# Attention with values as the moving operand and a column of ones, in a fused attention and soft mixture-of-experts kernel

## The chip, the cores and the metric

The kernel runs on one core of one Trainium2 chip. A core has five engines that run their own instruction streams in order: PE (TensorE, matrix multiply, writes PSUM only), DVE (VectorE), ACT (ScalarE), POOL (GpSimd, no access to PSUM) and SP (SyncE, which here only issues DMAs). The metric is device microseconds of one execution. In the profile PE is the stream of matmuls and PEld the stream of their weight loads, which run beside them.

## The reference

`q`, `k`, `v` are 8 batches x 8 heads x 576 positions x 64. Attention is done per head, then a soft mixture of experts on all 4608 rows:

```python
q_rot, k_rot = rotate(q), rotate(k)                  # rotary embedding
scores = 1/8 * q_rot @ k_rot.T                       # 576 x 576 per head
attn = exp(scores - max(scores, -1))
attn = attn / (sum(attn, -1) + 1e-9)
x = (attn @ v) -> rows (4608, 512)
logits = x @ phi                                     # 32 slots
d = softmax over rows (logits); c = softmax over slots (logits)
slot_input = d.T @ x                                 # 32 x 512
h = relu(slot_input[e] @ w1[e]); slot_out = h @ w2[e]
out = c @ slot_out
```

## The kernel before, in words

Two heads of one batch make a pair: head 0 on partitions 0 to 63, head 1 on 64 to 127. There are 32 pairs, four to a batch. For each pair these steps run, and the steps of several pairs overlap:

- `load0`, `load1` (SP): q and k of the pair, transposed, into `x_in` (two buffers). `spin` (POOL, 8 instructions): multiply by cosines and sines. `join` (DVE): add the two products. `high` (ACT, 2 instructions) and `low` (DVE): split into two f16 parts, `hl`. `low` is the last reader of `x_in`, so the load of the pair after next waits for it.
- `m00` to `m31` and `m_rem`: nine units that find the largest score of each query. PE computes scores from the high parts, DVE takes the maximum (L177, L185). `m_min` (DVE), `m_turn` (PE transposes, L200), `m_half` (ACT) and `m_rows` (a DMA) bring the negated maximum into a row, `peak`.
- `t0` to `t8`: nine score units. A unit is 64 keys x 576 queries of both heads in four terms (three products of the f16 parts, and the maximum through the constant `lift`), 16 matmuls of 64x64 stationary by 288 moving columns. ACT takes the exponential into `a_t` (L226).
- `av0` to `av8`: nine value units. Stationary is 64 keys x 64 columns of `v` in f32, moving is `a_t`, 288 columns. The result has head columns on partitions and queries along the row.
- `total`: the sums of the exponentials. DVE adds two groups of `a_t` into `c_t` (L252), PE multiplies by a 0/1 matrix `pick` (L263, 48 matmul passes of 128x32 stationary by 144 columns), ACT copies out (L269).
- `send`, `recip`, `spread`, `widen`: the sums go through small DMAs and DRAM to be spread over partitions, `norm` (POOL, L297) multiplies. The last two pairs do it on PE and DVE instead (`sums_turn`, `sums_wide`, L317, `norm_wide`).
- `natural` (PE, five transposes, L331 and L332) and `natural_out` (ACT) bring the rows into natural order, `xn`. Per batch: `logits` (L346), softmax statistics and the slot sums (L389 to L427).

Score units, maximum units, transposes and the like share three PSUM buffers of two banks (`ps_s`); the value result has one (`ps_o`).

The order on PE, ACT, DVE, SP and POOL is written out. `WHEN` gives every step of a pair a time in quarters of a pair; step s of pair p stands at `WHEN[s] + 4 * p`, and each engine takes its instructions in that order. A fixed list starts the first two pairs. Weights of the experts are loaded into free memory on the way; after the last pair come the statistics of the last batch, both expert layers and the output.

In PE's tables below 64\*64 or 128\*32 is rows x columns of the stationary tile. An f32 matmul is two passes, each with its own weight load, and each pass is one instruction in the profile.

Of the kernel before, what the change touches and what calls it, by code (L numbers as in the profile page):

```python
# [43 lines left out]
RC = 12  # L44
QC = HC // 2
PIECE = 4
NB = S // 64
GRP = 3
N_A = 3
WHEN = {  # L50
    "load0": -14.036, "load1": -13.155, "spin0": -11.12, "spin1": -11.002, "join": -8.686, "high0": -8.581,
    "high1": -8.145, "low": -7.119, "m01": -6.438, "m10": -6.296, "m00": -5.409, "m11": -4.37, "m21": -4.235,
    "m20": -3.955, "m30": -3.558, "load_v": -3.19, "m31": -2.689, "m_rem": -2.154, "m_min": -1.862, "m_turn":
# [5 lines left out]
    "recip": 4.894, "sums_wide": 5.348, "norm_wide": 5.483, "spread": 6.496, "natural_late": 6.717,  # L59
    "logits_late": 6.765, "logits_out_late": 6.993, "widen": 7.249, "natural_out_late": 7.405, "norm": 9.097,  # L60
    "natural": 11.079, "natural_out": 11.153, "logits": 11.213, "logits_out": 11.274, "stats": 12.331,
}
QL, QH, KH, KL = range(4)


@with_exitstack
# [884 lines left out]
```

## Time and profile before

| | |
|---|---|
| three runs | 551.47, 549.48, 551.17 us, median 551.17 |
| profiled execution | 549.75 us, span 548.0 us |
| busy PE, DVE, ACT, POOL | 515.7, 429.7, 311.6, 326.4 us |
| mean granted clock of PE | 0.98 |
| DMA | 111.35 MB, mean 203 GB/s |

A busy PE is not yet a PE at its limit, since an instruction lasts until its result is out while the next ones already stream: four 64\*64 matmuls of 288 columns last 0.29 us each, but a new set of four starts every 0.12 us. So the tables are read by the distance from start to start.

### The profile page before, as it was taken

The numbers are of one execution on the slowest core, as the hardware profiler recorded it, in microseconds if no ns is written. First come the engines' busy times: TensorE is split into PE (matmuls) and PEld (weight loads), VectorE is DVE, ScalarE is ACT, GpSimd is POOL, SyncE is SP. The second block draws the span as 40 slices with busy tenths as digits, with TensorE's granted clock in tenths as the row PEclk, the third lists the DMA queues.
The fourth block names the chain that finished last, engine by engine and source line by source line (L and its number), as shares of the span: only waits on it lengthen the run. The fifth ranks groups of instructions, "written<-read, shape, count | busy, mean of one in ns | idle before, by whom it ended". The sixth has DMA issues, their size and how long they took to land.

```text
span 548.0 us, 25344 instructions
## 1 busy us (share of the span) xinstructions
PE 515.7 (94%) x11325; PEld 389.2 (71%) x11325; DVE 429.7 (78%) x580; ACT 311.6 (57%) x655; POOL 326.4 (60%) x324
## 2 busy tenths in 40 slices
PE   4679999999999999999999999999999999999982
PEld 2267787877787777777887788777878886754551
DVE  5779998879998999899988998899889953232352
ACT  2146566666666666656675666566656665354441
POOL 1957787666886688668876887687678111210000
PEclk9689999999999999999999999999999999999997
DMA  7264566666566566556655665566434256459998
GB/s 263 93 216 134 193 194 193 193 192 193 194 194 193 192 192 195 190 183 202 196 195 159 220 197 195 169 204 206 138 120 121 70 182 218 169 190 411 407 417 343
DMA packets 51292, 111.35 MB, mean 203 GB/s; under 512 B 11504, under 2 KB 28656, under 8 KB 51184
## 3 DMA queue, kind: packets, MB, share of 16 engines
q1 hardware_dynamic: 51170, 109.73, 59.7%
q8 instruction: 89, 1.46, 1.1%
q14 instruction: 19, 0.16, 0.1%
q10 hardware_dynamic: 14, 0.00, 0.0%
HBM read 99.93 MB, written 9.58 MB: 200 GB/s over the span
## 4 chain that ended last, share of the span: by engine, by line
PE 87%; DVE 6%; DMA 4%; ACT 1%; issue 1%; SPq 0%; DVEq 0%; ACTq 0%
PE o_ps L238 26%; PE s_ps L225 26%; PE s_ps L263 9%; PE s_ps L175 6%; PE s_ps L331 3%; PE s_ps L789 3%; PE s_ps L346 2%; DVE nm L177 2%; DMA w_exp<-in_w 2%; PE s_ps L400 1%; PE s_ps L813 1%; PE s_ps L200 1%; DVE x_in L146 1%; DMA out<-w_exp 1%; PE s_ps L183 1%; DMA x_in<-in_qk 1%
## 5 line engine op out<-in xcount | busy, mean ns | idle before, releaser
L142 POOL TENSOR_TENSOR x_in<-x_in,cs_sb 128x288 f32<-128x288 f32 x248 | 254.5, 1063 | 80.8 <-DMA x_in<-in_qk 69.0
L226 ACT ACTIVATE a_t<-s_ps 128x576 f32<-128x576 f32 x288 | 179.6, 653 | 89.5 <-PE s_ps L225 89.2
L177 DVE TENSOR_REDUCE nm<-s_ps 128x2 f32<-128x576 f32 x256 | 183.0, 750 | 41.3 <-PE s_ps L175 39.5
L238 PE MATMUL o_ps<-a_t,v_in 64*64 64x288 f32 x2304 | 195.8, 408 | 0.0
L225 PE MATMUL s_ps<-hl 64*64 64x288 f16 x3456 | 166.5, 285 | 4.1 <-DVE nm L177 3.2
L225 PEld LDWEIGHTS <-hl 64*64 64x64 f16 x3456 | 124.6, 107 | 29.4 <-issue 6.5
L225 PE MATMUL s_ps<-peak,lift 64*64 64x288 f16 x1152 | 99.8, 284 | 0.3 <-issue 0.3
L238 PEld LDWEIGHTS o_ps<-a_t,v_in 64*64 64x64 f32 x2304 | 85.7, 133 | 8.2 <-issue 0.5
L175 PE MATMUL s_ps<-hl 64*64 64x288 f16 x1024 | 79.6, 290 | 4.1 <-DVE nm L177 4.0
L297 POOL TENSOR_TENSOR xt<-xt,rb 128x576 f32<-128x576 f32 x30 | 48.0, 1599 | 32.2 <-ACT a_t L226 13.1
L252 DVE TENSOR_TENSOR c_t<-a_t 128x1728 f32<-128x1728 f32 x32 | 62.8, 1961 | 0.0
L155 DVE TENSOR_TENSOR hl<-x_in,hl 128x1152 f16<-128x1152 f32 x32 | 60.1, 1880 | 0.5 <-ACT hl L151 0.5
L175 PEld LDWEIGHTS <-hl 64*64 64x64 f16 x1024 | 38.3, 106 | 24.7 <-issue 15.5
L146 DVE TENSOR_TENSOR x_in<-x_in 128x1152 f32<-128x1152 f32 (+2 forms) x36 | 55.3, 1535 | 0.1
L151 ACT CAST hl<-x_in 128x576 f16<-128x576 f32 (+1 forms) x66 | 40.1, 653 | 23.5 <-DVE x_in L146 21.6
L225 PEld LDWEIGHTS <-lift 64*64 64x64 f16 x1152 | 46.5, 107 | 0.7 <-issue 0.5
L337 ACT COPY xn<-s_ps 128x512 f32<-128x512 f32 x31 | 18.1, 583 | 29.1 <-PE s_ps L332 29.1
L420 POOL TENSOR_TENSOR ln<-ln,cm 128x160 f32<-128x160 f32 x7 | 14.7, 2096 | 32.4 <-DVE cm L419 32.4
L269 ACT ACTIVATE s<-s_ps,bits 128x144 f32<-128x144 f32 x32 | 12.2, 381 | 34.6 <-ACT xn L338 14.2
L263 PE MATMUL s_ps<-c_t,pick 128*32 128x144 f32 x768 | 30.4, 289 | 0.7 <-DVE c_t L252 0.5
L263 PE MATMUL s_ps<-a_t,pick 128*32 128x144 f32 x768 | 29.7, 286 | 0.0
L263 PEld LDWEIGHTS s_ps<-c_t,pick 128*32 128x32 f32 x768 | 21.1, 109 | 6.3 <-issue 4.7
(175 smaller groups left out, 463.7 us busy)
## 6 DMA issues: line engine op xcount, KB each, us to landing
x_in<-in_qk SPq DMA_DIRECT2D x62, 576.0 KB
w_exp<-in_w SPq DMA_DIRECT2D x63, 512.0 KB
v_in<-in_v SPq DMA_DIRECT2D x32, 576.0 KB
out<-w_exp SPq DMA_DIRECT2D x18, 512.0 KB
rb<-r_row SPq DMA_DIRECT2D x60, 144.0 KB
x_in<-in_qk SPq DMA_DIRECT2D x4, 288.0 KB
cs_sb<-in_cs SPq DMA_DIRECT2D x2, 288.0 KB
wk<-in_w SPq DMA_DIRECT2D x1, 512.0 KB
```

The lines of the kernel that those rows point to most:

```text
L142: eng.tensor_tensor(out=x[:, :, c], in0=x[:, :, c], in1=cs_sb[:, :, c], op=ALU.mult)
L146: nc.vector.tensor_tensor(out=x[:, t, 0, c], in0=x[:, t, 0, c], in1=x[:, t, 1, c], op=ALU.add)
L151: nc.scalar.copy(out=halves[p][:, 1 + t, c], in_=loaded[p][:, t, 0, c])
L155: nc.vector.tensor_tensor(out=hl[:, 0:4:3], in0=x[:, :, 0], in1=hl[:, 1:3], op=ALU.subtract)
L175: nc.tensor.matmul(s[rows[c ^ h], h, 0:HC], lhsT=hl[rows[h], QH, at:at + 64], rhs=hl[rows[h], KH, half[n]], start=True, stop=True)
L177: nc.vector.tensor_reduce(out=nms[p][:, n, j:8:4], in_=s[:, :, 0:HC], axis=AX.X, op=ALU.max, negate=True)
L225: nc.tensor.matmul(s[rows[h ^ n], n, 0:HC], lhsT=lhs, rhs=rhs, start=(x == 0), stop=(x == 3))
L226: nc.scalar.activation(out=ats[p, g][:, b].rearrange("p (n x) -> p n x", n=2), in_=s[:, :, 0:HC], func=AF.Exp, scale=SCALE)
L238: nc.tensor.matmul(o[rows[h], n, 0:HC], lhsT=vt[r, i, n], rhs=ats[p, g][r, b, half[n]], start=(i == 0), stop=(i == NB - 1))
L252: nc.vector.tensor_tensor(out=c, in0=ats[p, 0], in1=ats[p, 1], op=ALU.add)
L263: nc.tensor.matmul(s[32 * k:32 * k + 32, 0, 0:QC], lhsT=pick[:, 16 * n:16 * n + NS], rhs=(c, a)[x // GRP][:, x % GRP, QC * k:QC * k + QC], ...
L297: eng.tensor_tensor(out=xts[p], in0=xts[p], in1=rbs.pop(p), op=ALU.mult)
```

## The change

- Scores and maxima: the stationary tile has 128 columns (128 keys, or 128 queries for the maxima) in place of two of 64, so a unit has half as many matmuls. A score unit is now 128 keys x 288 queries; t0 to t7 cover 512 keys, t8 (`score_rest`) the last 64 keys in 64x64 tiles, with queries cut 320/256.
- Values: `a_t` (64 queries) is stationary and `v` moves, 64 columns and a column of ones, so that column 64 of the result is the sum of the exponentials. Units av0 to av3 are 128 keys deep (128\*64 tiles, 18 matmuls of 65 columns, two column halves), av4 is the last 64 keys (64\*64 tiles, 18 matmuls). The result has queries on partitions.
- `total`, `send`, `spread`, `widen` and their DMAs, the sum on DVE and the PE path of the last two pairs go. `o_out` is three ACT copies, `recip` three small DVE instructions, `norm` two POOL instructions that write `xn` directly. `natural` transposes `xn` to `xt` (five transposes of 128x128), for the logits only.
- `v` is laid out as 10 blocks of 65 columns on the host (325 KB a pair in place of 576 KB). `xn` has two buffers.
- All times in `WHEN` are new; the fixed start is now the table `EARLY` with the same steps. After the last pair `norm_last` divides straight from PSUM.

```diff
-    "load0": -14.036, "load1": -13.155, "spin0": -11.12, "spin1": -11.002, "join": -8.686, "high0": -8.581,
+    "load0": -13.475, "spin0": -13.456, "load1": -13.036, "spin1": -12.384, "join": -11.941, "high0": -11.78,
...
+    both = (slice(0, P),) if WIDE else rows
...
-        for c in range(2):
+        for c in both:
             for h in range(2):
-                at = P * j + 64 * (c ^ h)
-                nc.tensor.matmul(s[rows[c ^ h], h, 0:HC], lhsT=hl[rows[h], QH, at:at + 64],
+                nc.tensor.matmul(s[c, h, 0:HC], lhsT=hl[rows[h], QH, P * j + c.start:P * j + c.stop],
                                  rhs=hl[rows[h], KH, half[n]], start=True, stop=True)
...
+        for x, (k, q) in enumerate(TERMS):
+            for c in both:
+                for h in range(2):
+                    lhs = lift[rows[h], c] if k is None else hl[rows[h], k, P * b + c.start:P * b + c.stop]
+                    rhs = pk[rows[h], half[n]] if k is None else hl[rows[h], q, half[n]]
+                    nc.tensor.matmul(s[c, h, 0:HC], lhsT=lhs, rhs=rhs, start=(x == 0), stop=(x == 3))
+        nc.scalar.activation(out=ats[p, b][:, :, half[n]], in_=s[:, :, 0:HC], func=AF.Exp, scale=SCALE)
...
-        for n in range(2):
-            for h in range(2):
-                r = rows[h ^ n]
-                nc.tensor.matmul(o[rows[h], n, 0:HC], lhsT=vt[r, i, n], rhs=ats[p, g][r, b, half[n]],
-                                 start=(i == 0), stop=(i == NB - 1))
+        def unit(lhs, c, h, u, v, stop=False):
+            nc.tensor.matmul(o[rows[c], h, 65 * u:65 * u + 65], lhsT=lhs, rhs=v, start=(i == 0 and u == first), stop=stop)
+
+        if i < NB:
+            first = 0
+            for c, h, u in [(c, h, u) for u in range(4) for h in range(2) for c in range(2)] + [(0, 0, 4), (1, 1, 4)]:
+                q = 256 if u == 4 else 64 * u + 320 * c
+                unit(at[:, h, q:q + 64], c, h, u, vt[:, 2 * i + h])
...
+        nc.scalar.copy(out=t.rearrange("p h u x -> p h (u x)")[:, :, 0:260], in_=o[:, :, 0:260])
+        for h in range(2):
+            nc.scalar.copy(out=t[0:64, h, 4], in_=o[rows[h], h, 260:325])
...
+        nc.vector.tensor_scalar_add(out=rr[:, :, 0:4], in0=t[:, :, 0:4, 64], scalar1=1e-9)
+        nc.vector.tensor_scalar_add(out=rr[0:64, :, 4], in0=t[0:64, :, 4, 64], scalar1=1e-9)
+        nc.vector.reciprocal(out=rr, in_=rr)
...
+        eng.tensor_tensor(out=xn[:, :, 0:4], in0=t[:, :, 0:4, 0:64],
+                          in1=rr[:, :, 0:4].unsqueeze(3).broadcast_to([P, 2, 4, 64]), op=ALU.mult)
+        eng.tensor_tensor(out=xn[0:64, :, 4], in0=t[0:64, :, 4, 0:64],
+                          in1=rr[0:64, :, 4].unsqueeze(2).broadcast_to([64, 2, 64]), op=ALU.mult)
```

On PE, in the middle of the kernel, this stood before: the last transpose of `natural` (L332), the per-batch logits (L346), `total` (L263) and the start of a maximum unit (L175).

```order
L332 MATMUL s_ps<-id_sb,xt 64x128
L346 MATMUL s_ps<-xt,phi_sb 32x128 x16
L346 MATMUL s_ps<-xt,phi_sb 32x64 x16
L263 MATMUL s_ps<-c_t,pick 32x144 x12
L263 MATMUL s_ps<-a_t,pick 32x144 x12
L175 LDWEIGHTS hl
L175 MATMUL s_ps<-hl 64x288
```

This stands there now: the end of a score unit (L226), a maximum unit (L177), a value unit av0 (L255), the transpose of the maxima (L201) and the next maximum unit.

```order
L226 MATMUL s_ps<-peak_100,lift 128x288
L177 LDWEIGHTS hl
L177 MATMUL s_ps<-hl 128x288
L177 LDWEIGHTS hl
L177 MATMUL s_ps<-hl 128x288
L255 MATMUL o_ps<-v_in,a_t 64x65 x18
L201 MATMUL s_ps<-id_sb,min_111 64x128
L177 LDWEIGHTS hl
L177 MATMUL s_ps<-hl 128x288
```

`total` is gone, and a value unit in 128\*64 tiles now stands between units in 64\*128 tiles. Before, score, maximum and value units all had 64\*64 tiles. In the steady part a batch of four pairs had 24 changes of tile shape on PE, six of them from 128\*128 to 128\*64 inside a group of transposes; now it has 47.

On DVE, in the start of the kernel, from `low` of the second pair (pair 1) on, this stood before. L155 is `low`, L146 is `join`, nm_274 are the maxima of pair 1, nm_473 those of pair 2; the last row is `join` of pair 3.

```order
L155 TENSOR_TENSOR hl<-x_in,hl 128x2x576
L146 TENSOR_TENSOR x_in<-x_in 128x2x576
L177 TENSOR_REDUCE nm_274<-s_ps 128x2 x3
L155 TENSOR_TENSOR hl<-x_in,hl 128x2x576
L177 TENSOR_REDUCE nm_274<-s_ps 128x2
L177 TENSOR_REDUCE nm_473<-s_ps 128x2 x2
L185 TENSOR_REDUCE nm_274<-s_ps 128x2
L193 TENSOR_REDUCE min_120<-nm_274 128x9
L252 TENSOR_TENSOR c_t<-a_t 128x1728
L177 TENSOR_REDUCE nm_473<-s_ps 128x2
L146 TENSOR_TENSOR x_in<-x_in 128x2x576
```

From the same `low` (now L157) on, this stands there now. L148 is `join`, nm_255 are the maxima of pair 1 and nm_311 those of pair 2; the last `join` shown is again that of pair 3.

```order
L157 TENSOR_TENSOR hl<-x_in,hl 128x2x576
L179 TENSOR_REDUCE nm_255<-s_ps 128x2 x2
L148 TENSOR_TENSOR x_in<-x_in 128x2x576
L179 TENSOR_REDUCE nm_255<-s_ps 128x2
L187 TENSOR_REDUCE nm_255<-s_ps 128x2
L157 TENSOR_TENSOR hl<-x_in,hl 128x2x576
L179 TENSOR_REDUCE nm_311<-s_ps 128x2 x2
L179 TENSOR_REDUCE nm_255<-s_ps 128x2
L148 TENSOR_TENSOR x_in<-x_in 128x2x576
L179 TENSOR_REDUCE nm_311<-s_ps 128x2 x3
L187 TENSOR_REDUCE nm_311<-s_ps 128x2
L195 TENSOR_REDUCE min_112<-nm_255 128x9
```

`join` of pair 3 stood behind the minimum of pair 1 and the sum of pair 0. It now stands ahead of four maxima of pair 2 and the minimum of pair 1, and in every later pair `join` of pair q+1 stands three maxima behind `low` of pair q.

## Rows read from the trace of the kernel before

**Rows 1.** The page's busy time by engine, the granted clock in 40 slices, and the chain of work that ended last by engine and by line.

```profile
PE 515.7 (94%) x11325; PEld 389.2 (71%) x11325; DVE 429.7 (78%) x580; ACT 311.6 (57%) x655; POOL 326.4 (60%) x324
PEclk9689999999999999999999999999999999999997
PE 87%; DVE 6%; DMA 4%; ACT 1%; issue 1%; SPq 0%; DVEq 0%; ACTq 0%
```

**Rows 2.** Busy time in stretches: us, then busy us and (instructions) of PE, PEld, DVE, ACT, POOL, the granted clock, DMA share, GB/s. First a stretch of the start, then one batch from `logits` to `logits` (L346), then the experts.

```profile
20.00:40.00 20.00, 14.79 (x233) 10.38 (x237) 13.27 (x17) 6.31 (x11) 12.78 (x16) 0.79 0.43 149
...
274.11:329.12 55.01, 55.01 (x1314) 43.63 (x1313) 50.27 (x66) 35.32 (x75) 43.04 (x41) 1.00 0.61 192
329.12:384.63 55.51, 55.22 (x1314) 43.38 (x1313) 50.26 (x66) 35.34 (x75) 43.02 (x41) 1.00 0.58 191
...
485.82:548.00 62.18, 49.47 (x501) 25.77 (x500) 19.86 (x35) 26.51 (x55) 2.61 (x3) 0.94 0.96 383
```

**Rows 3.** PE's matmuls in order of time over one pair without per-batch work: start us, length us, engine, line, operation, tile, shape, count.

```profile
315.59 0.66 PE L331 MATMUL s_ps<-id_sb,xt 128*128 128x128 f32 x4
316.29 0.94 PE L263 MATMUL s_ps<-c_t,pick 128*32 128x144 f32 x24
317.05 0.92 PE L263 MATMUL s_ps<-a_t,pick 128*32 128x144 f32 x24
317.90 0.32 PE L175 MATMUL s_ps<-hl 64*64 64x288 f16 x4
...
318.53 0.29 PE L175 MATMUL s_ps<-hl 64*64 64x288 f16 x4
318.65 0.54 PE L225 MATMUL s_ps<-hl 64*64 64x288 f16 x12
...
319.14 0.29 PE L175 MATMUL s_ps<-hl 64*64 64x288 f16 x4
319.26 0.65 PE L238 MATMUL o_ps<-a_t,v_in 64*64 64x288 f32 x8
319.75 0.55 PE L225 MATMUL s_ps<-hl 64*64 64x288 f16 x12
...
324.68 0.68 PE L238 MATMUL o_ps<-a_t,v_in 64*64 64x288 f32 x8
325.16 0.31 PE L183 MATMUL s_ps<-hl 64*64 64x288 f16 x2
325.20 0.46 PE L238 MATMUL o_ps<-a_t,v_in 64*64 64x288 f32 x2
...
327.48 0.25 PE L200 MATMUL s_ps<-id_sb,min 64*64 64x64 f32 x2
328.42 0.44 PE L331 MATMUL s_ps<-id_sb,xt 128*128 128x128 f32 x2
```

**Rows 4.** The same columns where `sums_wide` (L317) of a late pair stands ahead of a value unit, and where 65-column f32 matmuls in 64\*64 tiles and 288-column f16 ones with 128 stationary columns stand.

```profile
462.54 1.22 PE L317 MATMUL s_ps<-id_sb,rn 72*64 72x72 f32 x32
463.69 1.20 PE L238 MATMUL o_ps<-a_t,v_in 64*64 64x288 f32 x16
...
479.36 1.16 PE L685 MATMUL o_ps<-acc,id_sb 64*64 64x65 f32 x64
...
481.08 0.65 PE L679 MATMUL s_ps<-peak,lift 128*128 128x288 f16 x4
```

**Rows 5.** The instructions of L317: duration ns least, median and most, first and last start.

```profile
L317 PE MATMUL s_ps<-id_sb,rn x64: 226/226/278, 462.5 to 477.0; 72*64 72x72 f32 x64
```

**Rows 6.** PE's per-batch work in order of time.

```profile
274.11 1.53 PE L346 MATMUL s_ps<-xt,phi_sb 128*32 128x128 f32 x64
275.45 0.92 PE L263 MATMUL s_ps<-c_t,pick 128*32 128x144 f32 x24
...
286.62 0.33 PE L389 MATMUL s_ps<-id_sb,d_t 128*128 128x128 f32 x1
286.99 0.25 PE L200 MATMUL s_ps<-id_sb,min 64*64 64x64 f32 x2
...
287.93 0.42 PE L397 MATMUL s_ps<-xn,dn 64*32 64x128 f32 x8
289.28 0.66 PE L331 MATMUL s_ps<-id_sb,xt 128*128 128x128 f32 x4
```

**Rows 7.** DVE, then POOL, in order of time over a pair; then `norm`-like products on POOL by line (duration ns least, median, most).

```profile
318.27 2.09 DVE L177 TENSOR_REDUCE nm<-s_ps 128x2 f32<-128x576 f32 x3
321.27 1.94 DVE L155 TENSOR_TENSOR hl<-x_in,hl 128x1152 f16<-128x1152 f32 x1
323.13 0.21 DVE L280 RECIPROCAL rr<-rc 96x12 f32<-96x12 f32 x1
326.52 1.95 DVE L252 TENSOR_TENSOR c_t<-a_t 128x1728 f32<-128x1728 f32 x1
...
315.10 8.77 POOL L142 TENSOR_TENSOR x_in<-x_in,cs_sb 128x288 f32<-128x288 f32 x8 [1.84 <-DMA x_in<-in_qk]
327.71 4.04 POOL L142 TENSOR_TENSOR x_in<-x_in,cs_sb 128x288 f32<-128x288 f32 x3 [2.48 <-DMA x_in<-in_qk]
...
L420 POOL TENSOR_TENSOR ln<-ln,cm x7: 2094/2096/2098, 135.0 to 464.9; 128x160 f32<-128x160 f32 x7
L427 POOL TENSOR_TENSOR cn_sb<-ln,cm x7: 453/457/468, 146.7 to 469.7; 128x160 f32<-128x160 f32 x7
```

**Rows 8.** The start: DVE's `low` of pair 1 and `join` of pair 3, POOL's `spin` of pairs 3 and 4, and PE's first score unit of pair 1.

```profile
28.22 1.35 DVE L155 TENSOR_TENSOR hl<-x_in,hl 128x1152 f16<-128x1152 f32 x1
43.08 1.34 DVE L146 TENSOR_TENSOR x_in<-x_in 128x1152 f32<-128x1152 f32 x1
...
12.68 13.55 POOL L142 TENSOR_TENSOR x_in<-x_in,cs_sb 128x288 f32<-128x288 f32 x16 [10.55 <-DMA x_in<-in_qk]
33.45 17.27 POOL L142 TENSOR_TENSOR x_in<-x_in,cs_sb 128x288 f32<-128x288 f32 x16 [7.22 <-DMA x_in<-in_qk]
...
44.99 0.54 PE L225 MATMUL s_ps<-hl 64*64 64x288 f16 x12
```

**Rows 9.** After the last value unit: ACT's copy of the result, then DVE's sum of the logits and its last copy into `xn`.

```profile
473.63 0.64 ACT L246 COPY xt<-o_ps 128x576 f32<-128x576 f32 x1
...
478.80 0.36 DVE L352 TENSOR_TENSOR l_sb<-s_ps,l_sb 128x192 f32<-128x192 f32 x1 [0.66 <-PE s_ps L346]
480.31 0.27 DVE L338 COPY xn<-s_ps 64x128 f32<-64x128 f32 x1
```

More of the change, by code (lines that the diff above doesn't have):

```diff
@@ L33 @@
 N_X = 5
+N_O = 2
 N_CS = 1
@@ L340, in logits, with natural_out @@
+        for j in range(5):
+            nc.tensor.transpose(t[:, P * j:P * j + P], xns[b][:, j, pp * P:pp * P + P], id_sb)
+    def natural_out(p, split=False):
+        xts[p] = xt = late.tile([P, S], F32, name="xt", bufs=N_X)
+        t = flat.pop(("n", p))
+        if split:
+            nc.scalar.copy(out=xt[:, 0:288], in_=t[:, 0:288])
+            nc.vector.tensor_copy(out=xt[:, 288:S], in_=t[:, 288:S])
+        else:
+            nc.scalar.copy(out=xt, in_=t[:, 0:S])
     def logits(*ps):
@@ L584, in attn_softmoe, with heat, small_loads, run @@
             plan[f"m{j}{n}"] = lambda p, j=j, n=n: m_unit(p, j, n)
-    for i in range(NB):
+    for i in range(2 * NB + 1):
         plan[f"t{i}"] = lambda p, i=i: score(p, i)
+    for i in range(NB + 1):
         plan[f"av{i}"] = lambda p, i=i: av(p, i)
-    done = set()
-    def do(name, p):
-        if (name, p) not in done and 0 <= p < NPAIR:
-            done.add((name, p))
-            plan[name](p)
-    beat = sorted((when % 4, int(when // 4), name) for name, when in WHEN.items())
+    def heat(n):
+        for _ in range(n):
+            nc.tensor.matmul(cold[:, 0, 0:HC], lhsT=lift, rhs=halves[0][:, KH, 0:HC], start=True, stop=True)
+    def small_loads(p):
+        nc.sync.dma_start(out=phi_sb, in_=phi.rearrange("(c p) n -> p c n", p=P))
+        nc.sync.dma_start(out=sel_sb, in_=sel)
+    plan.update({
+        "heat": lambda p: heat(16),
+        "small_loads": small_loads,
+        "join0": lambda p: join(p, 0),
+        "join1": lambda p: join(p, 1),
+    })
+    done = set()
+    def run(n, q):
+        if (n, q) not in done:
+            done.add((n, q))
+            plan[n](q)
     load(0)
@@ L611, in attn_softmoe @@
             high(0, t, c)
-    o = bank2()
-    def heat(n):
-        for i in range(n):
-            nc.tensor.matmul(o[:, 0, 0:HC], lhsT=lift, rhs=halves[0][:, KH, 0:HC], start=True, stop=True)
+    done.update((n, 0) for n in ("spin0", "spin1", "join", "high0", "high1", "load0", "load1"))
+    done.add(("join", 1))
+    cold = bank2()
     heat(N_WARM)
-    low(0)
-    done.update((n, 0) for n in ("spin0", "spin1", "join", "high0", "high1", "low", "load0", "load1"))
-    do("load0", 2)
-    do("load1", 2)
@@ L662, in attn_softmoe @@
-    p = NPAIR - 1
-    while later:
-        trickle(p)
-    while pending:
-        step(p)
-    release_stk()
-    for _, name in sorted((when, name) for name, when in WHEN.items()):
-        if name in plan and WHEN[name] <= WHEN["o_out"]:
-            do(name, p)
+    last = NPAIR - 1
+    events = [(when + 4 * q, n, q) for n, when in WHEN.items() for q in range(NPAIR)
+              if q < last or when < WHEN["o_out"]]
+    events = sorted([e for e in events if e[1:] not in EARLY] + [(when, n, q) for (n, q), when in EARLY.items()])
@@ L671, in attn_softmoe @@
+    for when, n, q in events:
+        if when >= 4 * NPAIR and ("flush", last) not in done:
+            done.add(("flush", last))
+            while later:
+                trickle(last)
+            release_stk()
+        run(n, q)
+        if (n, q) == ("low", last):
+            release_io()
+    p = last
     steady.close()
```

312 lines of the change are left out of this document (113 added, 199 removed), and 11 rows, old and new, of tables (EARLY, WHEN).

## The prediction

> **What bounds the kernel now.** I read the page's summary first, then the busy time by stretch, then PE's matmuls from start to start, then DVE and POOL beside them. PE is busy 94% of the span and carries 87% of the chain that ended last [rows 1]; in a batch of the middle it has no idle time (55.01 of 55.01 us) at the full granted clock, while DVE is busy 50.3 us, POOL 43 and ACT 35 [rows 2]. So what counts there is how long PE's stream is from start to start. From the first transpose of one pair to that of the next is 12.83 us (315.59 to 328.42). Inside it a maximum unit takes 0.12 us, a score unit 0.49 (318.65 to 319.14), a value unit 0.49 (319.26 to 319.75) and `total` 1.61 (316.29 to 317.90) [rows 3]. The tail after 485.8 us has its DMA engines 96% busy at 383 GB/s [rows 2]; the change leaves its bytes alone, so it only starts earlier or later.
>
> The one-run sum is made against the profiled execution, 549.75 us, of which the span is 548.0. The median of the runs is 551.17, 1.4 us above it; I add that difference at the end.
>
> **Scores and maxima.** The same products are done, in half as many matmuls. No row has 64\*128 tiles. The nearest is the 128\*128 one with 288 f16 columns: four take 0.65 us and one 0.29, so one starts every 0.12 us with its 128-column weights loaded beside it [rows 4]. If the two row halves run together, a term of a unit is 0.12 us as four 64\*64 tiles are now, and eight units of 0.49 plus the uneven last one (320 in place of 288 columns, 0.55) cost 4.47 us in place of 4.41. If they did not run together, scores and maxima would double, by 5 us a pair. I take the first: today both row halves already write the same PSUM partitions in the same 0.12 us [rows 3]. Cost: 0.06 us.
>
> **Values.** Per unit now 18 f32 matmuls of 65 columns in 128\*64 tiles, that is 36 passes, two at a time. `sums_wide` is nearly this: 32 passes of 72 columns in 72\*64 tiles, and 1.15 us to the next instruction [rows 4]. Its last pass starts 1.22 - 0.23 = 0.99 us after the first [rows 4, 5], so a round of two takes 0.062 after a first one stretched by 0.05, and from the end of the last round to the next shape 0.095 us pass. That gap is the price of a change of tile shape. With 65 columns a round is 0.057, a unit 18 x 0.057 + 0.05 = 1.08, with the gap behind it 1.17. The last unit in 64\*64 tiles has ten rounds; 64 such passes, 16 rounds, took 1.16 - 0.22 = 0.94 us [rows 4], 0.059 a round, so 0.64 with the stretched first. Together 4 x 1.17 + 0.64 = 5.32 in place of 9 x 0.485 = 4.37: plus 0.95.
>
> The Trainium skill, page "TensorE: Matmul & The Clock Gate", section LDWEIGHTS, gives a weight load as its columns divided by 1.2 per ns, 53 ns for 64. Two loads one after the other would make a round 107 ns and the values 3.6 us a pair longer, which speaks against a design with so many small stationary tiles. The trace disagrees: `sums_wide` loads two 64-column tiles in each round of 62 ns [rows 4]. I keep the row.
>
> **`total` and its followers.** 1.61 us of PE go [rows 3], with 1.95 us of DVE for `c_t` and 0.21 for the reciprocal [rows 7]. Three small DVE operations come, some 0.6 us by the 0.21 of L280. DVE is lighter by 1.5 us a pair, which costs or gives PE nothing by itself: PE waits for DVE nowhere in this pair. What PE loses is in one stretch: from 324.68 to 327.48 it does three value units, `m_rem` (0.12) and two score units, 2.56 us by their single times, with the gap of 0.095 before the transpose 2.65, and takes 2.80 [rows 3]. The 0.15 are where instructions of one unit stand two and two among those of the next, and the four tiles no longer start together. `m_rem`, the last value unit and the last score unit still follow each other in 64\*64 tiles, so I let half of it go: -0.07.
>
> **Changes of tile shape.** Three more entries into value units from score or maximum units, one into the last, two transitions of the transposed maximum and one back from the 64-column part: 5 x 0.095 and six first rounds stretched by 0.024 (144-column rounds of 0.122 follow a first of 0.147 now, as 24 passes of L263 take 0.76 from start to start and not 0.73 [rows 3]), together 0.62 us. A batch goes from 24 changes to 47.
>
> **A pair in the middle:** 0.06 + 0.95 - 1.61 + 0.62 = +0.02, less 0.07: -0.05 us, 31 times, -1.5 us. Three score buffers are shared as before, and runs of four score units can wait for exponentials. The ends of this term are -0.25 (nothing lost, cheaper first rounds) and +0.3 a pair, -8 and +9 us.
>
> **A batch** costs 55.3 - 4 x 12.83 = 4.0 us beyond its pairs [rows 2, 3]. `logits` keeps its 1.34, the slot sums 1.35 (287.93 to 289.28) [rows 6]. The two groups of transposes cost 0.37 each plus a change of shape (286.62 to 286.99) and now follow `natural`, which has the same shape; 0.27 each. With one change less around the slot sums, -0.55 us, seven times: -4 us.
>
> **ACT and POOL.** `o_out` is three ACT copies and `natural_out` one in place of two, the exponentials are as many elements; ACT's 35 us of 55 hide it. `norm` on POOL is 640 elements with a broadcast operand. L427, the same kind, takes 0.457 us for 160, so 1.8 us in place of 1.4; L420 takes 2.1 for 160, which would be 8.4 [rows 7]. I take L427, a product into another tile as here.
>
> **The start.** In the old order `join` of pair 3 stood last, at 43.08, and PE was full by then [rows 8]. Now it stands ahead of four maxima of pair 2, whose PSUM buffers PE needs, as the order of DVE's instructions shows. `low` of pair 1 stays at 28.22, and the load and `spin` behind it start at 33.45; eight of the sixteen POOL products last 8.6 us at that rate, 6.8 at that of the first sixteen (13.55) [rows 8], so `join` can start between 40.2 and 42.1. DVE gets to it at about 37 (28.22 + 1.35 + two operations of 1.35 + seven maxima of 0.7), PE has then done four score units of pair 0 and stops. From the end of `join` (41.6 to 43.5) PE still has about 7 us (three score units, `t8`, three value units with their gaps, seven maxima) before the first score unit of pair 1, which comes at 49 to 51 and not 44.99. It is a further 1.5 us behind in values of pair 0 and 1.1 ahead in maxima. PE's clock in this stretch is 0.79 on average [rows 2]; a stop could keep it low a little longer. Bounds 0 and +9; I take +5.5 us, since PE never has slack later to win it back.
>
> **The end.** From the last copy of values to the summed logits is 5.2 us now, through the sums on PE and DVE [rows 9]. `norm_last` takes two small copies, three small DVE operations, a product from PSUM, five transposes, a copy and the logits, about 4.7 by rows of like size, and `xn` is no longer what comes last (480.31). -1 us. The sum: -1.5 - 4 + 5.5 - 1 = -1, so 548.75 for an execution like the profiled one, 550.2 beside the median. I take the middle, 549.5.
>
> **Rivals.** (a) *The start costs little and waits vanish.* If spins run at their fast rate and `join` is early, the start loses 2, and pairs win 0.25: -8 - 4 + 2 - 1 = -11, 540. For it: DVE has 1.5 us more room. Against: `join` of pair 3 cannot beat its load. (b) *`join` waits for POOL in every pair*, slower. It now stands three maxima (2.09 us) behind `low` of the pair before, so from the end of `low` that frees the buffer there are 12.83 + 2.09 = 14.9 us. Load to the first `spin` takes 4.5 (323.21 to 327.71), `spin` 8.77 [rows 7], 13.3 together: 1.6 us to spare, where before it was 5. If `spin` or `norm` between two spins takes 2 us more than that, each pair grows by 0.4: +12, 561. (c) *PE has more buffer waits* than I left, +0.25 a pair: +8 more, 557. (d) *The change does not do what it says for the tiles*: row halves one after the other, +5 a pair, about 700; or `norm` at L420's rate, POOL at 17 us a pair, +4 a pair, about 675.
>
> **How the numbers follow.** About 0.5% (2.75 us) is what a measurement of this kernel can tell from no change. My sum has 0.50, between 542 and 556: 0.22 of it faster, 0.25 within 0.5%, 0.03 slower. (a) 0.18, all faster; (b) 0.12 and (c) 0.14, slower but for 0.03 within 0.5%; (d) 0.06, slower. That is faster 0.40, same 0.28, slower 0.32. The range, 536 to 562, leaves out (d) and the ends of the others.
>
> **What will show it.** Right: rounds of 64\*128 tiles 0.12 us apart; value units of 1.08 us and gaps of 0.095; 12.8 us a pair; PE idle at 38 to 42 us; the first score unit of pair 1 at 49 to 51. Wrong: DVE idle at `join` in each pair (b), PE idle for exponentials or maxima in each pair (c), rounds of 0.24 us or POOL without idle time (d).

## The result and the profile after

The changed kernel takes 553.62 us (median of 20 runs, 551.23 to 558.07), the kernel before 550.30 in the same series; the ratio is 1.0067, with a 95% interval of 1.0047 to 1.0087. So it is slower by about 0.67% (3.7 us by the ratio, 3.3 by the medians), and I had forecast 549.5, a little faster than before. The profiled executions differ as much: spans of 551.3 and 548.0 us.

The page of the changed kernel, against [rows 1]: busy time, the granted clock in 40 slices of 13.8 us, and the chain of work that ended last.

```profile
PE 510.1 (93%) x10420; PEld 376.9 (68%) x10420; DVE 366.0 (66%) x610; ACT 313.2 (57%) x688; POOL 283.3 (51%) x356
PEclk9657999999999999999999999999999999999997
PE 84%; DVE 5%; DMA 5%; POOL 1%; ACT 1%; issue 1%; SPq 0%; ACTq 0%; DVEq 0%; POOLq 0%
```

PE has 5.6 us less to do, and DVE 64 us less. What is worse is in the second to fourth slice: the clock is 6, 5, 7 tenths there, before it was 6, 8, 9.

The stretches that answer to [rows 2] (columns: us, then busy us and instructions of PE, PEld, DVE, ACT, POOL, granted clock, DMA share, GB/s): the start, two batches from `logits` to `logits` (now L342), the experts.

```profile
20.00:40.00 20.00, 11.14 (x71) 6.40 (x73) 13.69 (x17) 4.13 (x7) 12.88 (x16) 0.59 0.34 119
287.10:341.43 54.33, 54.33 (x1230) 42.10 (x1229) 42.32 (x70) 35.63 (x80) 35.85 (x44) 1.00 0.45 154
341.43:396.50 55.07, 54.48 (x1229) 42.04 (x1228) 41.16 (x70) 35.51 (x80) 37.49 (x46) 1.00 0.40 132
489.06:551.30 62.24, 49.55 (x501) 25.82 (x500) 19.86 (x35) 26.47 (x55) 2.63 (x3) 0.94 0.94 373
```

A batch is 0.4 to 0.7 us shorter than in [rows 2], the experts take 62.24 us in place of 62.18, and at the start PE does 11.14 us of work where it did 14.79. So the middle has won what it was to win, and the loss lies at both ends.

Where exactly can be read from one instruction that stands once in every pair at the same place: the transpose of the minima (`m_turn`). PE's rows of it for pair 1 and pair 31, first in the kernel before, then in the changed one.

```profile
41.08 0.25 PE L200 MATMUL s_ps<-id_sb,min 64*64 64x64 f32 x2
...
452.57 0.25 PE L200 MATMUL s_ps<-id_sb,min 64*64 64x64 f32 x2
```

```profile
48.96 0.30 PE L201 MATMUL s_ps<-id_sb,min 128*64 128x128 f32 x1
...
454.31 0.30 PE L201 MATMUL s_ps<-id_sb,min 128*64 128x128 f32 x1
```

Up to pair 1 the changed kernel loses 48.96 - 41.08 = 7.9 us. The thirty pairs between take 405.35 in place of 411.49 us: 6.1 won. From pair 31 to the end of the span it is 97.0 in place of 95.4: 1.6 lost. Together 3.3. Two limits of this split: the same order of the middle takes 404.3 to 407.9 us in the profiles of the runs below, so the 6.1 is good to some 2 us. And the mark does not stand behind the same work: ahead of it in pair 1 the new order has done three score units and 1.7 us of values less than the old one and five maximum units more, in all some 2.6 us less of PE's work by the prices of single units (an estimate), so the loss at the start is rather above 7.9 and that at the end rather below 1.6. Their sum does not hang on the mark.

The start, against [rows 8]: DVE's `join` of pair 3 (L148), then PE's rows behind it, up to the first score unit of pair 1 at 53.27.

```profile
40.53 1.93 DVE L148 TENSOR_TENSOR x_in<-x_in 128x1152 f32<-128x1152 f32 x1 [3.19 <-POOL x_in L144]
```

```profile
43.18 0.42 PE L177 MATMUL s_ps<-hl 64*128 64x288 f16 x2 [2.17 <-DVE nm L179]
...
45.55 0.90 PE L226 MATMUL s_ps<-hl 64*128 64x288 f16 x6
...
46.49 0.45 PE L177 MATMUL s_ps<-hl 64*128 64x288 f16 x2
46.87 2.17 PE L255 MATMUL o_ps<-v_in,a_t 128*64 128x65 f32 x36
48.96 0.30 PE L201 MATMUL s_ps<-id_sb,min 128*64 128x128 f32 x1
...
53.27 0.54 PE L226 MATMUL s_ps<-hl 64*128 64x288 f16 x6
```

DVE stands 3.19 us at `join` and PE waits behind it. The score unit at 45.55 takes 0.94 us to the next instruction and the value unit at 46.87 takes 2.09; in the middle these are 0.50 and 1.20. The granted clock there (columns as above) is 0.50, the lower of the two levels, 1.2 GHz, and in the second stretch it rises to the full one just before 49 us.

```profile
40.00:45.00 5.00, 2.58 (x28) 1.68 (x26) 4.36 (x5) 1.79 (x3) 5.00 (x6) 0.50 0.00 0
45.00:50.00 5.00, 5.00 (x71) 3.44 (x64) 1.64 (x4) 1.67 (x4) 2.62 (x4) 0.62 0.00 0
```

The end, against [rows 9]: PE's last value unit and first expert, then ACT between them.

```profile
473.93 0.81 PE L255 MATMUL o_ps<-v_in,a_tr 64*64 64x65 f32 x36
...
489.06 2.34 PE L729 MATMUL s_ps<-w_exp,slot_t 128*32 128x512 f32 x18
```

```profile
475.47 0.64 ACT L334 COPY xt<-s_ps 128x576 f32<-128x576 f32 x1 [2.57 <-PE s_ps L325]
476.99 0.32 ACT L350 COPY l_sb<-s_ps 128x192 f32<-128x192 f32 x1 [0.88 <-PE s_ps L342]
477.21 0.46 ACT L429 CAST csp<-cn_sb 128x320 fp32r<-128x320 f32 x1
477.57 0.43 ACT L311 COPY odd<-o_ps 64x65 f32<-64x65 f32 x2
```

The values are complete at 473.93 + 0.81 = 474.74, but ACT's two copies with which the last normalisation begins (L311) start at 477.57. Before them in ACT's queue stand pair 30's transposes (L334), the logits of pairs 28 to 30 (L350), which wait for PE, and a cast.

### The profile page after: what moved, and what is told of

The parts are those of the page before. It is cut to its first block, busy times and chain, and to the rows that moved or that the text cites. A ratio compares the mean times of both kernels' runs of the same rounds, so it can differ in the third digit from the quotient of the medians.

```text
span 551.3 us, 23417 instructions
## 1 busy us (share of the span) xinstructions
PE 510.1 (93%) x10420; PEld 376.9 (68%) x10420; DVE 366.0 (66%) x610; ACT 313.2 (57%) x688; POOL 283.3 (51%) x356
## 4 chain that ended last, share of the span: by engine, by line
PE 84%; DVE 5%; DMA 5%; POOL 1%; ACT 1%; issue 1%; SPq 0%; ACTq 0%; DVEq 0%; POOLq 0%
PE o_ps L255 31%; PE s_ps L226 23%; PE s_ps L177 7%; PE s_ps L325 4%; PE s_ps L240 3%; PE s_ps L729 3%; PE s_ps L342 2%; DVE nm L179 2%; DMA w_exp<-in_w 2%; PE s_ps L185 2%; DMA x_in<-in_qk 2%; PE s_ps L201 1%; PE s_ps L396 1%; POOL x_in L144 1%; PE s_ps L753 1%; DMA out<-w_exp 1%
## 5 line engine op out<-in xcount | busy, mean ns | idle before, releaser
L144 POOL TENSOR_TENSOR x_in<-x_in,cs_sb 128x288 f32<-128x288 f32 x248 | 198.1, 833 | 103.0 <-DMA x_in<-in_qk 90.0
L179 DVE TENSOR_REDUCE nm<-s_ps 128x2 f32<-128x576 f32 x256 | 184.6, 754 | 76.9 <-PE s_ps L177 75.2
L227 ACT ACTIVATE a_t<-s_ps 128x576 f32<-128x576 f32 x256 | 153.5, 653 | 129.6 <-PE s_ps L226 129.4
L255 PE MATMUL o_ps<-v_in,a_t 128*64 128x65 f32 x4608 | 163.0, 225 | 0.7 <-ACT a_t L227 0.7
L255 PEld LDWEIGHTS o_ps<-v_in,a_t 128*64 128x64 f32 x4608 | 145.5, 138 | 26.5 <-issue 21.1
L226 PE MATMUL s_ps<-hl 64*128 64x288 f16 x1536 | 134.0, 286 | 2.9 <-DVE nm L179 2.5
L226 PEld LDWEIGHTS <-hl 64*128 64x128 f16 x1536 | 71.2, 95 | 32.3 <-issue 15.1
L226 PE MATMUL s_ps<-peak,lift 64*128 64x288 f16 x512 | 74.4, 286 | 1.1 <-DMA peak<-mr 1.1
L177 PE MATMUL s_ps<-hl 64*128 64x288 f16 x512 | 65.8, 293 | 9.4 <-DVE nm L179 6.9
L301 POOL TENSOR_TENSOR xn<-o_sb,rr 128x512 f32<-128x512 f32 x31 | 48.3, 1558 | 34.8 <-DVE rr L293 33.4
L148 DVE TENSOR_TENSOR x_in<-x_in 128x1152 f32<-128x1152 f32 (+2 forms) x36 | 46.5, 1291 | 3.3 <-POOL x_in L144 3.2
L157 DVE TENSOR_TENSOR hl<-x_in,hl 128x1152 f16<-128x1152 f32 x32 | 44.9, 1402 | 0.5 <-ACT hl L153 0.5
L177 PEld LDWEIGHTS <-hl 64*128 64x128 f16 x512 | 25.4, 95 | 25.8 <-issue 10.5
L226 PEld LDWEIGHTS <-lift 64*128 64x128 f16 x512 | 25.7, 95 | 7.7 <-issue 1.3
L187 DVE TENSOR_REDUCE nm<-s_ps 128x2 f32<-128x576 f32 x32 | 24.3, 759 | 5.2 <-PE s_ps L185 5.0
L255 PEld LDWEIGHTS o_ps<-v_in,a_tr 64*64 64x64 f32 x1152 | 21.5, 134 | 7.5 <-issue 7.4
L255 PE MATMUL o_ps<-v_in,a_tr 64*64 64x65 f32 x1152 | 26.0, 224 | 0.0
```

The lines of the kernel that those rows point to most:

```text
L144: eng.tensor_tensor(out=x[:, :, c], in0=x[:, :, c], in1=cs_sb[:, :, c], op=ALU.mult)
L148: nc.vector.tensor_tensor(out=x[:, t, 0, c], in0=x[:, t, 0, c], in1=x[:, t, 1, c], op=ALU.add)
L157: nc.vector.tensor_tensor(out=hl[:, 0:4:3], in0=x[:, :, 0], in1=hl[:, 1:3], op=ALU.subtract)
L177: nc.tensor.matmul(s[c, h, 0:HC], lhsT=hl[rows[h], QH, P * j + c.start:P * j + c.stop], rhs=hl[rows[h], KH, half[n]], start=True, stop=True)
L179: nc.vector.tensor_reduce(out=nms[p][:, n, j:8:4], in_=s[:, :, 0:HC], axis=AX.X, op=ALU.max, negate=True)
L226: nc.tensor.matmul(s[c, h, 0:HC], lhsT=lhs, rhs=rhs, start=(x == 0), stop=(x == 3))
```

## The experiments

All times are medians beside runs of the kernel before on the same chip; a ratio of 1.0067 is the changed kernel. Two ratios that differ by less than about 0.003 are not told apart. The edits add lines near the top, so line numbers of the pairs move by some three to six; the names in the rows stay. In the diffs a table entry sets the place of a step in the order, four units to a pair.

### Which wait at the start costs

Scores first:

```diff
+EARLY.update({
+    ("t0", 0): -4.6, ("t1", 0): -4.4, ("t5", 0): -3, ("t6", 0): -2.6,
+})
```

> Only the order at the start changes: four score units of pair 0 (t0, t1, t5, t6) stand ahead of the maxima m21, m20, m30 and m_rem of pair 1. Theory A (the start's loss is PE standing behind maximum units that wait for DVE, the waits of 1.6, 2.5 and 1.8 us at 30 to 36 us): these waits get filled with scores, the first score unit of pair 1 comes at 47 to 50 us in place of 53.3, and the time falls by 3 to 6 us, to about 549. Theory B (the loss is the wait for `join` of pair 3 alone): that wait stays at 37 to 41 us, and the time falls by 1 us or less. Theory C (the loss lies in the tail and the pairs): no change.

Measured: 552.71 us, 1.0048 [1.0027, 1.0068]. The gain of 1 us is within the noise, and the first score unit of pair 1 comes at 52.58, 0.7 us earlier: theory A alone is refuted, B is not. `join` late:

```diff
+EARLY.update({
+    ("join", 3): 2.05, ("high0", 3): 2.06, ("high1", 3): 2.07,
+})
```

> Only `join` of pair 3 (DVE) and its two f16 copies (ACT) move back, from 0.06 to 2.05 in the table, behind the last maxima of pair 1. Theory A: PE still stands behind DVE before 36 us, but the 2.2 us wait at 43 goes, so 1 to 3 us. Theory B (the step as I predicted it: `join` blocks DVE and costs 5.5 us): the time falls by 5 us or more. Theory C: no change.

Measured: 550.38 us, 1.0000 [0.9977, 1.0022]. That is 0.67% below the changed kernel, 3.7 us: between A and B. The rows of `join` on DVE and of the score unit on PE:

```profile
41.90 1.52 DVE L151 TENSOR_TENSOR x_in<-x_in 128x1152 f32<-128x1152 f32 x1
```

```profile
48.39 0.54 PE L229 MATMUL s_ps<-hl 64*128 64x288 f16 x6
```

`join` waits for nothing now, and pair 1's scores start 4.9 us earlier. Both edits together, with no other:

> The scores of pair 0 ahead of pair 1's maxima, and `join` of pair 3 behind them, both together; nothing else. Theory A (two stops stand one behind the other, and taking away the first only moves PE's waiting to the second, as the 0.9 us of the first alone say): together they give more than the sum of the two alone (0.9 and 3.2 us), 5 to 7 us, about 547. The rival (the maxima that DVE has to do in any case set the end of the start): together no more than `join` alone, about 550.5.

Measured: 548.75 us, 0.9971 [0.9946, 0.9995], 0.96% or 5.3 us below the changed kernel. The transpose of pair 1's minima stands at 42.96, so 6.0 of the 7.9 us are back. Theory A asked for more than the sum of the two alone, and that is not shown: by the ratios the two alone gave 1.0 and 3.7 us, and neither their sum nor `join` alone (1.0000 against 0.9971) is told apart from both together. In the profiles the transpose stands at 48.26 with the scores first and at 43.65 with `join` late, 0.7 and 5.3 us earlier, which is the 6.0. So there are two stops, and what they give adds up.

### Does the clock cost, or the wait?

Matmuls of `lift` and a zeroed tile, results unused, where PE waits, first 8, 12, 8 and 10 of them, then 34 in the last place:

```diff
+        "hot3": lambda p: hot(34),
...
+    ("hot0", 0): -2.69, ("hot1", 0): -0.58, ("hot2", 0): -0.1, ("hot3", 0): 0.3,
```

> The order is that of the changed kernel; 38 matmuls of 288 columns whose result is not used are put where PE waits at 30, 33, 36 and 42 us. The theory of the clock (a large part of the loss is that PE, having waited, runs at 1.2 GHz until 48 us): the granted clock is 1.0 from about 36 us on and the time falls by 2 to 5 us though nothing waits less. The rival (PE only waits for DVE and POOL there, whatever its clock): the clock rises, the waits get longer by as much, and the time stays within 1 us; if the extra matmuls get in the way, it rises by up to 3 us.

Measured: 553.64 us, 1.0070 [1.0043, 1.0098]. Nothing won, but the windows of this run (columns as above) show that the test was not complete:

```profile
40.00:45.00 5.00, 1.43 (x23) 0.93 (x22) 4.39 (x5) 1.79 (x3) 5.00 (x6) 0.99 0.00 0
45.00:50.00 5.00, 5.00 (x72) 3.43 (x67) 1.94 (x5) 2.08 (x5) 2.71 (x4) 0.67 0.01 3
```

PE still stood idle while `join` waited, and its clock was down again just behind that (0.67). So the longer one:

> As the first run with extra matmuls, but 34 of them and not 10 while PE waits for `join` of pair 3. In the first one the clock was 1.0 from 25 to 45 us, yet PE stood idle from 39.9 to 43.3 and was back at 0.67 from 45 to 50. If the step that I sized too low is PE's work behind `join` (I counted 7 us from rows at the full clock, and it took 10.8): the clock stays at 1.0 from 40 to 55, the first score unit of pair 1 comes at about 50 us and not 53, and the time falls by 2 to 3 us below the changed kernel, to 551. The rival (what follows `join` is paced by DVE and ACT, and the clock does not matter): first score unit at 52.5 or later, and no change.

Measured: 553.95 us, 1.0067 [1.0040, 1.0094]. The same windows, and the first score unit of pair 1:

```profile
40.00:45.00 5.00, 4.98 (x56) 3.51 (x55) 4.64 (x6) 2.05 (x4) 5.00 (x7) 1.00 0.00 0
45.00:50.00 5.00, 5.00 (x115) 3.89 (x111) 3.38 (x6) 2.50 (x6) 2.28 (x4) 1.00 0.10 21
```

```profile
50.87 0.54 PE L229 MATMUL s_ps<-hl 64*128 64x288 f16 x6
```

The clock is full from 30 us on and the unit comes 2.4 us earlier, as the theory said; the time does not follow. With both intervals a gain of up to some 1.9 us could hide, 2.4 hardly. Where it is given back the one profile does not say: there the transpose of pair 31's minima is still 1.7 us ahead, and the profiled execution is one of the faster of its seven (552.03 us). The Trainium skill, page "TensorE: Matmul & The Clock Gate", section "HAM oscillation — how this bites in real kernels", counts as the penalty the throttled time times (1 - 1.2/2.4). By that this run, with a mean granted clock of 0.983 against 0.965 in the profiled executions, would be worth some 10 us, an estimate: 0.018 more on average means 2 x 0.018 x 551 = 20 us less at the lower level, and half of that. By the medians of all runs, 0.980 and 0.968, it is 6.6. The measured gain is 0.0 us, give or take 1.9. A reason that fits is that PE was waiting for much of that time whatever its clock (from 40 to 45 us it was busy 2.58 of 5 us in the changed kernel); no run shows it by itself. Such matmuls in the best order, which comes below, six ahead of `t6` and two behind each of five maxima:

> The best order so far (the three edits together, 546.2) with 16 unused matmuls between the maxima that wait for DVE from 31 to 40 us. If the clock is what is left at the start: 1.0 instead of 0.5 to 0.79 from 30 to 45 us, and 1 to 1.5 us less, about 545. The rival (DVE's maxima set the pace): the same 546, or more where the extra matmuls stand in the way.

Measured: 546.62 us, 0.9948 [0.9927, 0.9969], against 0.9936 without: the rival held.

### The place in ACT's queue at the end

```diff
+        if (n, q) == ("natural_out", last - 1):
+            norm_last(last)
         run(n, q)
...
-    norm_last(p)
     keep(9)
```

> Only the order at the end changes: the normalisation of the last pair is issued ahead of the copy of pair 30's transposes, so ACT does its two small copies first. In the changed kernel they start 2.8 us after the last value matmul (474.7 to 477.57). If the end's loss is this place in ACT's queue, the normalised values are there 2.5 us earlier and the time falls by 2 to 2.7 us. The rival (the sum of the small operations on the way is simply longer than the old way through the sums): the copies start earlier but the logits of pairs 28 to 30, pushed back, come last, and the time falls by under 1 us.

Measured: 551.39 us, 1.0036 [1.0019, 1.0052]: 2.2 us less by the medians, 1.7 by the ratios, at the edge of what is told apart. ACT's first copy and the first expert in this run, whose values are complete at 476.06:

```profile
476.09 0.43 ACT L311 COPY odd<-o_ps 64x65 f32<-64x65 f32 x2 [1.88 <-PE o_ps L255]
```

```profile
488.51 2.34 PE L730 MATMUL s_ps<-w_exp,slot_t 128*32 128x512 f32 x18
```

From the last value to the experts it is 12.45 us, where it was 489.06 - 474.74 = 14.32. So 1.9 of the 2.8 us at ACT come back. `xn` is done at 477.96, but its transposes on PE start at 479.29, behind the logits of pairs 28 to 30 and nine matmuls (L632) whose result is not used.

### Start and end together

First `join` late and this edit, then the scores first as well; nothing new in either.

> `join` of pair 3 late, and the last normalisation ahead of the copy of pair 30's transposes. If the losses at the start and at the end are two places that have nothing to do with each other, the gains add up: 3.2 and 2.2 us, to about 548, 0.3% below the kernel before. The rival (what comes earlier waits at the end for the weights of the experts, whose transfer keeps the DMA engines busy there): about 550, as with `join` alone.

Measured: 547.63 us, 0.9963 [0.9939, 0.9986]. The gains add.

> The three edits of order that gave something alone, together: scores of pair 0 ahead of pair 1's maxima, `join` of pair 3 behind them, and the last normalisation ahead of the copy of pair 30's transposes. If start and end are independent, the gains add: 4.9 of the two at the start and 2.2 at the end, from 553.6 to 546.5, 0.6% below the kernel before. The rival (what is won at the start waits at the end for the expert weights): 547.6 as without the scores, or more.

Measured: 546.16 us, 0.9936 [0.9910, 0.9962]. With these three edits of the order the changed kernel is 0.6% faster than the kernel before. Whether that one would gain by such edits at its own start and end was not tried.

### More work between the maxima

Here `t8`, `t4`, `t7`, `t3` and three value units of pair 0 were put between the maxima of pair 2, and the minima of pair 1 with their way to the peak rows were put earlier.

```diff
+    ("t8", 0): -0.5, ("t4", 0): -0.4, ("m_min", 1): 0.1, ("av0", 0): 0.15, ("t7", 0): 0.2, ("m_turn", 1): 0.24,
+    ("m_half", 1): 0.26, ("av2", 0): 0.28, ("t3", 0): 0.33, ("m_rows", 1): 0.6, ("av3", 0): 2.7,
```

> As the three edits together, and the last score unit, t4, t7 and t3 of pair 0 with three of its value units stand between the maxima of pair 2, which DVE works off from 34.7 to 40 us while PE waits for buffers. If DVE's maxima set the pace there and PE has 3 us of work to put beside them, 2 to 3 us less, about 544. The rival (DVE, POOL and the loads set when pair 3 and 4 are ready, and PE waits for these later instead): 546 to 547, with new waits at 45 to 60 us.

Measured: 549.04 us, 0.9986 [0.9965, 1.0008], slower than without. SP's queue, where the peak rows (L216) now stand ahead of the loads of pair 4 at 41.71:

```profile
29.91 1.21 SPq L145 DMA_DIRECT2D x_in<-in_qk  x2
40.33 0.65 SPq L216 DMA_DIRECT2D peak<-mr  x1
...
41.71 0.98 SPq L145 DMA_DIRECT2D x_in<-in_qk  x2
```

The rows waited for ACT, and the loads behind them. With the rows left where they were:

```diff
-    ("m_half", 1): 0.26, ("av2", 0): 0.28, ("t3", 0): 0.33, ("m_rows", 1): 0.6, ("av3", 0): 2.7,
+    ("m_half", 1): 0.26, ("av2", 0): 0.28, ("t3", 0): 0.33, ("av3", 0): 2.7,
```

> As the weave of scores and values between the maxima of pair 2, but the rows of the peaks of pair 1 stay behind the loads of pair 4 in SP's queue, where they are in the changed kernel. In the weave they had been put ahead of these loads, which then went out at 41.7 us and not at 29.7 to 35.8, and `join` of pair 4 waited 3.96 us for POOL. If that queue is what spoilt it: the loads go out by 36 us, `join` of pair 4 stands at 47 to 49, and the time is 543 to 545, below the three edits alone (546.2). The rival (by then POOL and DVE, not PE, set the pace of the first pairs): 546 or more.

Measured: 547.86 us, 0.9975 [0.9952, 0.9998]. `join` of pair 4 stands at 49.76 without a wait, but the time is not below 0.9936, nor told apart from the run before it (0.9986). The stop at the queue is gone in the profile, and another has come, as the rival said: at 46.51 PE waits 1.66 us for ACT's copies of pair 3, since DVE comes to `join` of pair 3 only at 43.63, when the maxima that PE delivered more slowly are done.

### What a change of tile shape costs

Order of the middle, two value units together twice in a pair:

```diff
+WHEN.update({"av2": 2.41, "t2": 3.99, "av1": 3.998})
```

> Order of the changed kernel, but in every pair two value units follow the one before them at once (av2 behind av0, t2 ahead of av3 and av1 behind it): some four changes of tile shape a pair fewer. If a change costs 0.095 us and a stretched first round 0.024, as I worked them out, 0.48 us a pair, 15 us in all, to about 538. The rival (the value units in between give ACT and DVE time to empty the three score buffers, and PE waits for them when it does more than four score units and maxima on end): the gaps go, but PE waits for exponentials and maxima instead, and the time is from 550 up.

Measured: 598.79 us, 1.0882 [1.0837, 1.0927]. PE's rows of two units together, and its waits by what it waited for (us in total, times, longest us):

```profile
302.51 2.32 PE L256 MATMUL o_ps<-v_in,a_t 128*64 128x65 f32 x72
304.76 0.30 PE L202 MATMUL s_ps<-id_sb,min 128*64 128x128 f32 x1
```

```profile
PE s_ps L227 <- DVE nm L180: 14.5, 30, 1.8
PE s_ps L178 <- ACT xt L335: 8.3, 27, 0.3
PE s_ps L227 <- ACT a_t L228: 7.6, 30, 0.5
PE s_ps L178 <- ACT a_t L228: 7.5, 31, 0.3
```

Two units take 2.25 and not 2.40 us, so a gap is saved, and 37.9 us of waits for the score buffers come in its place (the same four rows come to 2.8 in the changed kernel). They are the larger part of the 45 us; the rest I have not assigned. Second, the transposed minima away from the value unit behind which they stand in the same tile shape:

```diff
+WHEN.update({"m_turn": -1.3, "m_half": -1.29})
```

> Order of the changed kernel, but the transpose of the minima, which stands behind a value unit in the same tile shape, moves behind the next maximum unit: two changes of tile shape a pair more, and no other work. By the prices of my working (0.095 us for the gap and 0.024 for a stretched first round) 0.19 to 0.24 us a pair, so 6 to 7.5 us in all, about 560. The rival (a gap of this kind is the time that the last matmul needs to get through, and PE loses it beside any other cause anyway): under 3 us, below 556.5.

Measured: 555.87 us, 1.0110 [1.0082, 1.0139], 0.43% or 2.4 us above the changed kernel: the rival held. Its rows:

```profile
317.92 1.27 PE L256 MATMUL o_ps<-v_in,a_t 128*64 128x65 f32 x36
319.12 0.29 PE L178 MATMUL s_ps<-hl 64*128 64x288 f16 x2
319.35 0.30 PE L202 MATMUL s_ps<-id_sb,min 128*64 128x128 f32 x1
319.58 0.54 PE L227 MATMUL s_ps<-hl 64*128 64x288 f16 x6
```

From the value unit's start to the next instruction it is 1.20 us whether a maximum unit in 64\*128 tiles follows, as here, or the transpose in the unit's own shape, as in the pair shown below. The gap is there in either case; moving the transpose costs about 0.1 us a pair in the profile and not 0.2. Third, scores and maxima in 64\*64 tiles again:

```diff
-WIDE = True
+WIDE = False
```

> Scores and maxima in 64*64 tiles again, twice as many matmuls in the same places of the order; everything else as in the changed kernel. My step (the two row halves of 64*128 tiles run together, a term takes 0.12 us either way, and only the changes of shape beside m_rem, t8 and the last value unit, which are in 64*64 tiles, fall away): a score unit stays 0.49 us, a pair loses 0.2 to 0.45 us, and the time falls by 6 to 14 us. The rival (the four 64*64 tiles of a term do not start together next to other shapes, or twice the weight loads cost something): a score unit of over 0.5 us, and the time equal or up to 10 us longer.

Measured: 568.70 us, 1.0340 [1.0282, 1.0398], 15 us above the changed kernel, which neither theory had forecast. A score unit in this run starts at 312.13 and the next unit at 312.62, 0.49 us as before. What is longer is in the chain of its page and in PE's waits:

```profile
PE 78%; DMA 9%; DVE 6%; issue 3%; POOL 1%; ACT 1%; SPq 0%; DVEq 0%; ACTq 0%; POOLq 0%
```

```profile
PE o_ps L255 <- issue: 5.8, 6, 2.1
...
PE s_ps L240 <- issue: 3.8, 4, 1.5
...
PE s_ps L226 <- issue: 2.1, 2, 1.4
```

Time in which PE waited for nothing that the profile shows is 3% of the span and not 1%, some 11 us more. (The larger share of DMA in the chain lies in the experts, and from pair 31's transpose to the end it takes 96.9 us here and 97.0 there, so it is not what is longer.) That the instructions themselves came late would fit (12980 matmuls and as many weight loads, against 10420), but it was not tried by itself.

## Why the prediction was wrong, step by step

**The middle was right.** One pair of the changed kernel, against [rows 3]:

```profile
316.51 1.27 PE L255 MATMUL o_ps<-v_in,a_t 128*64 128x65 f32 x36
317.71 0.30 PE L201 MATMUL s_ps<-id_sb,min 128*64 128x128 f32 x1
...
319.86 1.27 PE L255 MATMUL o_ps<-v_in,a_t 128*64 128x65 f32 x36
321.06 0.54 PE L177 MATMUL s_ps<-hl 64*128 64x288 f16 x6
...
322.74 0.54 PE L226 MATMUL s_ps<-hl 64*128 64x288 f16 x6
...
323.24 0.53 PE L226 MATMUL s_ps<-hl 64*128 64x288 f16 x6
...
330.45 0.30 PE L201 MATMUL s_ps<-id_sb,min 128*64 128x128 f32 x1
```

A score unit takes 0.50 us (predicted 0.49), a value unit with its gap 1.20 (1.17), the pair 12.74 (12.78). The two row halves run together, and two weight loads fit into each round, so of the two prices for weight loads that the prediction weighed, the one of the row was the one to keep. Pairs and batches were to give 5.5 us; 6.1 came. The price of a change of tile shape, one of the terms, was named wrongly in one place at least: the gap behind a value unit is as long ahead of the transpose, in the same shape, as the moved transpose shows. What causes it stays open. The sum came out all the same, since the value unit with its gap costs nearly what the term said; that the wrong name did the sum no harm is luck.

**The start was sized too low**: +5.5 predicted, +7.9 measured by the transposes. The first score unit of pair 1 came 53.27 - 44.99 = 8.3 us later, where 4 to 6 had been predicted. `join` started at 40.53 (predicted 40.2 to 42.1), DVE stood idle at it and PE behind it, as said. The step that failed is "from the end of `join` PE still has about 7 us": it took 53.27 - 42.46 = 10.8, since I had taken the units at the prices of the middle, while PE ran at 1.2 GHz until almost 49 us, and had left out the 0.7 us until DVE's first maximum behind `join` frees a buffer for PE (43.18). With the clock held up it is 50.87 - 42.09 = 8.8, of which PE's stream takes 7.6 from where it begins (43.29). What the clock costs in whole time is another matter: the run with the clock held up was no faster, while `join` moved away gave 3.7 us. And I had looked only at `join`. The four maxima ahead of pair 0's first scores are a second and smaller stop, 0.7 us at the transposes whether `join` is in the way or not. The 1.9 us that are left of the 7.9 no run assigns.

**The end had the wrong sign**: -1 predicted, +1.6 measured from pair 31's transpose on. From the last value to the experts it is 14.32 us, where it was 485.82 - 473.63 = 12.2 from ACT's copy behind the last value [rows 2, 9]: 2.1 lost, and 0.6 won ahead of that. This stretch does not hang on the mark of the transposes. "About 4.7 by rows of like size" for the last normalisation is right from where it begins: 477.57 to 482.09, the sum of the logits, is 4.5 us. What failed is that I let it begin at once. ACT's queue holds it back for 2.8 us, because the new order puts pair 30's transposes and logits behind the last values; issued ahead of them it begins 0.03 us after the last value. The rest of the -1, from `xn` no longer being what comes last, came to nothing: from the sum of the logits to the experts it is 489.06 - 482.09 = 6.97 us, and it was 485.82 - 478.80 = 7.02.

**The sum**: -1 predicted, +3.3 measured, so 4.3 us off; by these marks 2.4 at the start and 2.6 at the end, less 0.6 in the middle. Without the miss at the end I would have been within what can be told from no change.

**The rivals.** (a) had POOL's fast rate right (a `spin` product takes 833 ns on average, 1063 before) and the cheap start wrong. (b) is out: DVE waited for POOL at `join` 3.2 us in the whole run, once, at the start. (c) is out in this order, though the grouped order shows how near it is. (d) is out: the score unit says so, and `norm` takes 1.56 + 0.57 = 2.1 us (predicted 1.8), far from the 8.4 of L420's rate.

## What to carry to other kernels

When a change moves work to another place in the order, price the first and the last few rounds by themselves: list what stands ahead of each step in every in-order queue there, down to small copies, and what those wait for. Here the 0.2 us won in each of thirty pairs, batches included, were nearly all lost again by one operation on DVE and two copies on ACT that stood behind a wait: with these moved, 5.7 us come back. And where two stops are found, take both away in one run as well as each alone: only that says whether their gains add, as these did (0.7 and 5.3 us of the transpose's place, 6.0 together), or whether one hides the other.

## What the runs showed of the chip that I had not expected

- A granted clock of 1.0 from 30 us on (0.983 over the whole run, not 0.965) made the first score unit of pair 1 2.4 us earlier and the kernel no faster that could be measured.
- The gap of about 0.1 us behind a value unit stands ahead of the transposed minima too, in the same tile shape; between two value units it is gone (2.25 us for two, against 1.20 for one).
- Scores and maxima in twice as many matmuls (12980 in place of 10420 in all, a score unit 0.49 us either way) took 15 us longer, of which the trace puts some 11 on PE waiting for nothing that it shows, in stops of up to 2.1 us. The cause is open.
- The products of `spin` on POOL became 22% shorter (833 and 1063 ns) though nothing in them changed. DVE has 64 us less to do, `c_t` above all, and the DMAs move less; which of these does it was not tried.
